# Seven products in five banks with two uses each, the mirrored tile's square first, x added on VectorE for two pairs

## The chip, the cores and the metric

The kernel runs on one core of one Trainium2 chip. The metric is the device time of one execution in microseconds (us). Engines are called by their short names: PE (TensorE, matmuls and transposes), ACT (ScalarE), DVE (VectorE), POOL (GpSimd, which here mostly issues transfers) and SP (SyncE, which issues transfers). Each engine works through its own instructions in order; semaphores tie the engines together. SBUF holds 128 partitions; PSUM, which PE writes to, is used in eight banks of 128 x 512 f32.

## The reference

A sequence x of 2048 rows and 1024 features goes through a Fourier mixing and an MLP, both modulated by a condition c:

```python
mod = (_silu(c) @ w_mod).reshape(c.shape[0], 6, 1, -1)
sa, ca, ga, sb, cb, gb = (mod[:, 0], mod[:, 1], mod[:, 2], mod[:, 3], mod[:, 4], mod[:, 5])
h = _layernorm(x, axis=-1) * (1 + ca) + sa
x = x + ga * _A_ref(h, ...)   # Re(DFT over rows and features)
h = _layernorm(x, axis=-1) * (1 + cb) + sb
x = x + gb * _B_ref(h, ...)
# _B_ref: layernorm, then gelu(y @ w1 + b1) @ w2 + b2, w1 is 1024 x 3584, w2 is 3584 x 1024
```

Everything is f32 at the interface. The part that the change touches is the middle: `x + ga * A`, the two layer norms that follow each other (that of `h` and that inside `_B_ref`), and the operands of the first MLP product.

## The kernel before, in words

The matrix products run in f16 with operands split into a high part (the value rounded to f16) and a low part (the rest). The MLP's products are not taken directly: seven sums and differences of blocks are multiplied for each weight group (a fast matrix product with seven products, m = 0 to 6, in place of eight). So for each group of rows seven operands have to be formed, each as a high and a low f16 tile.

The order of the instructions is fixed by a planner that runs in Python while the kernel is built. Work is cut into `Task`s with an engine, a cost, dependencies and a key. They stand in streams, and the planner always takes the stream head that can start first by its own clocks. `LANDS` says how long after its issue it takes a transfer for done (`("st", "xa")`, an accumulating transfer that adds x, 8.0 us), `LAGS` what it adds for a handover, `due` which stream comes first. These numbers move instructions; they wait for nothing on the chip, where semaphores decide.

The 2048 rows are worked on as 16 row tiles, in 8 pairs b = 0 to 7. Of a pair, tile n = 0 lies in plain order, tile n = 1 in mirrored order, which is read and written by indirect transfers (helpers at L2168 for reading and L2171 for writing, both on POOL). Three pair buffers y and w are used in turn, so pair b uses those of pair b - 3. For each pair (`ln2`):

1. PE makes the Fourier products (L3079 and L3091), DVE brings them to y (L3100, L3105).
2. y is multiplied by ga on DVE (L3211). Then x is added: by an accumulating transfer that POOL issues (mirrored tile through L2168, the other by L3216). For the pairs in `ADDED` (0, 6 and 7) x is loaded into w beforehand (SP at L3164 and POOL through L2168), and DVE multiplies (L3207) and adds (L3208). The sum is stored out, by L2171 for the mirrored tile and on SP at L3223 for the other.
3. The squares on ACT (L3185), DVE's L3233, roots on ACT (L2628, L2629) with a few short DVE steps (L2634 to L2637), DVE's L3237, squares again (L3185), roots again, L3244, and the final L3246 on ACT, which leaves the normalised rows in w.
4. `z_psum` (pairs 0 to 6): PE turns blocks of w into PSUM banks 3 to 7 (L3366), ACT writes the high part of an operand (L3386), DVE the low part (L3414, or L3416 with a factor), and PE adds further blocks into a bank with matmuls by the unit matrix (L3373). For two of the seven, m = 5 and 6, PE subtracts the high part in the bank (L3423) and ACT writes the rest (L3429). For pairs 4 to 6 the operands are kept aside by transfers from POOL (L3405).
5. Pair 7 is turned whole: PE transposes (L3256) into banks 6 and 7, ACT copies out (L3265, L3263).

In `z_psum` the banks before are: 3 and 4 for m = 0 and 1, which are used once; 5 for m = 5; 6 and 7 for m = 3 and 4; and 7 again for m = 2 and once more for m = 6. So bank 7 has three uses in a chain.

Some products of gemm3 (the first MLP matrix; 12 matmuls each at L3860, ACT's L4177 and L4173, DVE's L4183) are put between these steps of the last pairs. After the last turning the two MLP matrices follow, group by group: L3860 is gemm3, L3974 gemm4, and ACT and DVE prepare the weights for them (L2396, L2408, L2422, L3514).

## Time and profile before

| | us |
|---|---|
| three runs, median (lowest to highest) | 1349.69 (1348.94 to 1349.77) |
| the profiled execution, its own time | 1349.1 |
| its span (first to last instruction) | 1347.3 |
| PE busy | 1234.3 |
| DVE busy | 1054.6 |
| ACT busy | 737.2 |
| end of pair 7's last L3246 | 334.1 |
| end of the last turning, L3256 | 344.9 |

1.8 us of the profiled time lie outside the span. A row of a timeline gives the start and the length of an instruction, then its engine, line and tiles, and in brackets how long its engine stood idle before it and what ended that. A row of the groups gives busy time and mean, then the idle time before the group's instructions by what ended it.

### The profile page before, as it was taken

Reading aid. Unit: us, or ns where it says so; the run is one execution under the profiler, and the core shown is the slowest. Engines: PE = TensorE matmul, PEld = TensorE weight load, DVE = VectorE, ACT = ScalarE, POOL = GpSimd, SP = SyncE. Lnnn points to the kernel's source line nnn. Section 1 sums busy time; section 2 is a strip of 40 time slices with the busy share of each in tenths; the row PEclk is TensorE's granted clock in tenths of the full one; section 3 lists DMA queues with packets and bytes.
Section 4 is the critical chain, followed back from the end, with each engine's and each line's share of the span. In section 5 each row is a group of like instructions: output and inputs, shape, how many; then the busy total and the mean of one; then the engine's idle time right before and its main releaser. Section 6 shows DMA issues by size and latency. Waiting matters only on the chain.

```text
span 1347.3 us, 16846 instructions
## 1 busy us (share of the span) xinstructions
PE 1234.3 (92%) x5923; PEld 581.8 (43%) x5923; DVE 1054.6 (78%) x1596; ACT 737.2 (55%) x1207; POOL 248.7 (18%) x380
## 2 busy tenths in 40 slices
PE   3658876679899999999999999999999999999997
PEld 1225434444444444444444444444444444444443
DVE  5789776876688999989899896567777868586785
ACT  4885645878767656474647251366455453526330
POOL 2000123222011000000000001345243242233101
PEclk9689798878899999999999999999999999999999
DMA  9966368776258868483634385968695766585155
GB/s 365 392 213 209 125 219 202 204 256 229 93 201 246 271 181 242 132 252 113 218 107 170 143 331 162 280 229 298 203 315 195 233 229 198 190 290 184 57 175 116
DMA packets 103686, 285.23 MB, mean 212 GB/s; under 512 B 13116, under 2 KB 13132, under 8 KB 101672
## 3 DMA queue, kind: packets, MB, share of 16 engines
q1 hardware_dynamic: 75304, 191.96, 40.9%
q0 software_dynamic: 28288, 92.10, 23.9%
q8 instruction: 48, 0.79, 0.2%
q14 instruction: 46, 0.38, 0.1%
HBM read 199.08 MB, written 84.93 MB: 211 GB/s over the span
## 4 chain that ended last, share of the span: by engine, by line
PE 71%; DVE 2%; ACT 1%; DMA 1%; issue 0%; SPq 0%; DVEq 0%
PE ps L3974 35%; PE ps L3860 35%; DVE arena L4024 1%; DVE arena L2408 1%; DMA arena<-in_w_dram 1%; ACT arena L2396 0%; DVE arena L2422 0%; ACT arena L4173 0%; DVE arena L4076 0%; ACT arena L4014 0%; PE ps L3256 0%; ACT arena L3879 0%; DVE arena L3886 0%; ACT L4173 0%; DVE arena L4071 0%
## 5 line engine op out<-in xcount | busy, mean ns | idle before, releaser
L3860 PE MATMUL ps<-arena 128*128 128x512 f16 x2352 | 514.5, 380 | 1.0 <-ACT arena L3882 1.0
L3974 PE MATMUL ps<-arena 128*128 128x512 f16 x2352 | 510.7, 379 | 2.0 <-DVE arena L4024 1.6
L3860 PEld LDWEIGHTS <-arena 128*128 128x128 f16 x2352 | 230.9, 98 | 281.8 <-issue 7.3
L3974 PEld LDWEIGHTS <-arena 128*128 128x128 f16 x2352 | 230.1, 98 | 280.3 <-issue 2.6
L4024 DVE SCALAR_TENSOR_TENSOR arena<-ps,i4c,arena 128x1024 f32<-128x1024 f32 x179 | 229.4, 1282 | 93.7 <-PE ps L3974 90.0
L2396 ACT ACTIVATE arena<-arena,shc 128x512 f16<-128x512 f32 (+1 forms) x115 | 116.1, 1017 | 129.8 <-DVE arena L2422 76.2
L2408 DVE SCALAR_TENSOR_TENSOR arena<-arena,shc 128x512 f16<-128x512 f32 (+1 forms) x115 | 128.9, 1122 | 35.6 <-ACT arena L2396 35.1
L3744 ACT ACTIVATE arena<-arena 128x512 f32<-128x512 f32 (+4 forms) x159 | 97.2, 613 | 108.1 <-DVE arena L3753 85.2
L2422 DVE TENSOR_TENSOR arena<-arena 128x512 f32<-128x512 f32 (+1 forms) x196 | 149.1, 765 | 3.9
L3879 ACT ACTIVATE arena<-arena,b1s,i1c 128x512 f32<-128x512 f32 x78 | 63.4, 813 | 91.1 <-DVE arena L3886 88.2
L2396 ACT ACTIVATE arena<-arena,s1c 128x512 f16<-128x512 f32 (+1 forms) x70 | 60.9, 886 | 68.1 <-DVE arena L2422 40.2
L3753 DVE TENSOR_TENSOR arena<-arena 128x256 f32<-128x256 f32 x240 | 88.0, 422 | 1.0 <-DMA arena<-in_cre_dram 0.8
L3886 DVE TENSOR_TENSOR arena<-arena,ps 128x512 f32<-128x512 f32 x78 | 53.4, 685 | 43.6 <-PE ps L3860 40.6
L3526 POOL PARTITION_ALL_REDUCE sums<-sums x21 | 9.7, 465 | 419.1 <-DVE sums L3522 407.3
L2408 DVE SCALAR_TENSOR_TENSOR arena<-arena,s1c 128x512 f16<-128x512 f32 (+1 forms) x70 | 65.8, 959 | 7.2 <-ACT arena L2396 7.0
L2408 DVE SCALAR_TENSOR_TENSOR arena<-arena,s2c 128x1024 f16<-128x1024 f32 x49 | 62.1, 1280 | 6.7 <-ACT arena L2396 6.6
L3882 ACT ACTIVATE arena<-ps 128x512 f32<-128x512 f32 x78 | 45.9, 589 | 36.0 <-PE ps L3860 36.0
L3514 ACT ACTIVATE ps<-arena 128x1024 f32<-128x1024 f32 x46 | 46.7, 1015 | 18.8 <-DMA arena<-in_w_dram 11.0
L2396 ACT ACTIVATE arena<-arena,s2c 128x1024 f16<-128x1024 f32 x49 | 55.1, 1138 | 1.5 <-DVE arena L2422 1.5
L3015 PE MATMUL ps<-arena 128*128 128x256 f16 (+5 forms) x297 | 43.8, 296 | 6.6 <-ACT arena L2794 3.2
L3790 POOL DMA_DIRECT2D arena<-in_cim_dram x69 | 38.0, 555 | 53.2 <-ACT arena L3744 28.9
L3185 ACT ACTIVATE arena<-arena,lns 128x1024 f32<-128x1024 f32 x32 | 36.5, 1142 | 20.1 <-DMA arena<-in_x_dram 9.8
(243 smaller groups left out, 1133.8 us busy)
## 6 DMA issues: line engine op xcount, KB each, us to landing
fw<-arena SPq DMA_DIRECT2D x71, 512.0 KB
arena<-fw SPq DMA_DIRECT2D x119, 256.0 KB
arena<-fw SPq DMA_DIRECT2D x49, 512.0 KB
arena<-in_wm_dram SPq DMA_DIRECT2D x32, 512.0 KB
arena<-in_w_dram SPq DMA_DIRECT2D x32, 512.0 KB
arena<-in_cre_dram POOLq DMA_DIRECT2D x64, 256.0 KB
arena<-in_cim_dram POOLq DMA_DIRECT2D x64, 256.0 KB
arena<-in_w_dram SPq DMA_DIRECT2D x56, 256.0 KB
```

Of the source, the lines that this page charges most:

```text
L2396: act.activation(o[m][0], q(j), AF.Copy, **sc)
L2408: dve.scalar_tensor_tensor(o[m][1], q(j), scale, o[m][0], op0=ALU.mult, op1=ALU.subtract)
L2422: dve.tensor_tensor(q(d), q(a), q(b), op=op)
L3514: act.activation(junk, parts[j][0], AF.Square, accum_out=t[:, j : j + 1])
L3744: f = lambda: act.activation(v, v, AF.Square, accum_out=csum[0:pn, n : n + 1])
L3753: return lambda: dve.tensor_tensor(dst[0][:, o::2], src[0][:, o::2], dst[0][:, o::2], op=op)
L3860: pe.matmul(ps.rearrange("p (k t) -> p k t", k=4), w1c[:, m, s, a, d * P : (d + 1) * P], zc(m)[:, b, :, d, :], start=(start and d == 0 and ...
L3879: act.activation(dst, src, AF.Gelu_apprx_tanh, scale=inv, bias=b1s[:, 2 * p + j : 2 * p + j + 1])
L3882: after_pe("act", 0.5, lambda: act.activation(quad(g)[:, n], ps[b], AF.Copy), kp[b])
L3886: after_pe("dve", 0.6, lambda: dve.tensor_tensor(q, q, ps[b], op=ALU.add), kp[b])
L3974: pe.matmul(t[:, j], hidc[:, c_, m, a, k * P : (k + 1) * P], w2c[:, m, c_, w], start=(start and c_ == 0 and n == 0), stop=(c_ == 1 and n = ...
L4024: lambda: dve.scalar_tensor_tensor(dst, ps[b], inv, dst, op0=ALU.mult, op1=ALU.add), kp[b],
```

## The change

The seven operands are now formed in five banks with two uses each: 3 and 4 hold m = 0 and 1, 5 holds m = 5, 6 and 7 hold m = 3 and 4; then m = 6 is made in bank 4 (m1 - m5 + m3) and m = 2 in bank 5 (m5 - m3), each from what still lies there. Four evictions on ACT and four on DVE take the place of seven and three; the path by L3423 and L3429 is gone, and so is the factor -1. Banks 6 and 7 are free once m = 3 and 4 are out, 4 and 5 once m = 6 and 2 are out. Pair 6 leaves `ADDED` and gets x by accumulating transfers. The first squares begin with the mirrored tile. For the planner an addition of x lands after 7.0 us, and not less than 2.8 us after the one before.

In the rows of the change, lines that lie behind the edits carry other numbers: L3216 is now L3218, L3246 L3248, L3256 L3258, L3263 and L3265 are L3265 and L3267, L3366 is L3368, L3373 L3376, L3386 L3389, L3405 L3408, L3414 L3416, L3860 L3843, L3974 L3957, L4173 L4156, L4177 L4160.

What POOL issues for pairs 1 to 4, of before. The rows are, from the top, pair 1's two additions (L2168 the mirrored tile, L3216 the other), pair 1's out-store, pair 2's additions and out-store, pair 3's additions, and pair 4's first:

```order
L2168 DMA arena_65<-in_x_dram,idxm_98 128x1024
L3216 DMA arena_65<-in_x_dram 128x1024
L2171 DMA out_dram<-arena_65,idxm_98 1024x1024
L2168 DMA arena_65<-in_x_dram,idxm_98 128x1024
L3216 DMA arena_65<-in_x_dram 128x1024
L2171 DMA out_dram<-arena_65,idxm_98 1024x1024
L2168 DMA arena_65<-in_x_dram,idxm_98 128x1024
L3216 DMA arena_65<-in_x_dram 128x1024
L2168 DMA arena_65<-in_x_dram,idxm_98 128x1024
```

and of the change:

```order
L2168 DMA arena_65<-in_x_dram,idxm_98 128x1024
L3218 DMA arena_65<-in_x_dram 128x1024
L2168 DMA arena_65<-in_x_dram,idxm_98 128x1024
L3218 DMA arena_65<-in_x_dram 128x1024
L2171 DMA out_dram<-arena_65,idxm_98 1024x1024 x2
L2168 DMA arena_65<-in_x_dram,idxm_98 128x1024
L3218 DMA arena_65<-in_x_dram 128x1024
L2171 DMA out_dram<-arena_65,idxm_98 1024x1024
L2168 DMA arena_65<-in_x_dram,idxm_98 128x1024
```

Pair 2's two additions have moved ahead of pair 1's out-store, and the two out-stores now stand together behind them.

What POOL issues for pairs 5 to 7, of before, where pair 5's additions are followed by its out-store, the load of pair 6's x, pair 6's out-store, and the load of pair 7's x:

```order
L2168 DMA arena_65<-in_x_dram,idxm_98 128x1024
L3216 DMA arena_65<-in_x_dram 128x1024
L2171 DMA out_dram<-arena_65,idxm_98 1024x1024
L2168 DMA arena_65<-in_x_dram,idxm_98 128x1024
L2171 DMA out_dram<-arena_65,idxm_98 1024x1024
L2168 DMA arena_65<-in_x_dram,idxm_98 128x1024
L3405 DMA fzc_67<-arena_65 256x1x512
```

and of the change:

```order
L2168 DMA arena_65<-in_x_dram,idxm_98 128x1024
L3218 DMA arena_65<-in_x_dram 128x1024
L2171 DMA out_dram<-arena_65,idxm_98 1024x1024
L2168 DMA arena_65<-in_x_dram,idxm_98 128x1024
L3218 DMA arena_65<-in_x_dram 128x1024
L2171 DMA out_dram<-arena_65,idxm_98 1024x1024
L3408 DMA fzc_67<-arena_65 256x1x512
L3408 DMA fzc_68<-arena_65 256x1x512
L3408 DMA fzc_72<-arena_65 256x1x512
L2168 DMA arena_65<-in_x_dram,idxm_98 128x1024
```

Pair 6's x is now a pair of additions, L2168 and L3218, behind pair 5's out-store, and the load of pair 7's x stands behind three transfers that keep operands aside.

ACT around the end of pair 7, of before: the last L3246, the evictions of pair 6's operands (L3386, L3429), gelus (L4173), weight preparation (L2396), and the copy of the first turned tile (L3265):

```order
L3246 ACTIVATE arena_65<-arena_65,lns_24_156 128x1024
L4173 ACT_TABLE_LOAD
L4173 ACTIVATE arena_65<-arena_65,b1s_158,i1c_162 128x512
L3386 ACTIVATE arena_65<-ps 128x512
L4173 ACTIVATE arena_65<-arena_65,b1s_158,i1c_162 128x512 x2
L4177 ACTIVATE arena_65<-ps 128x512
L3386 ACTIVATE arena_65<-ps 128x512
L4173 ACTIVATE arena_65<-ps,b1s_158,i1c_162 128x512
L3429 ACTIVATE arena_65<-ps 128x512
L4173 ACTIVATE arena_65<-arena_65,b1s_158,i1c_162 128x512
L2396 ACTIVATE arena_65<-arena_65,s2c_165 128x2x512
L3265 ACTIVATE arena_65<-ps 128x1024
```

and of the change, from the first L3248 of pair 7 to the copy of the second turned tile (L3265):

```order
L3248 ACTIVATE arena_65<-arena_65,lns_24_156 128x1024
L3389 ACTIVATE arena_65<-ps 128x2x512
L4160 ACTIVATE arena_65<-ps 128x512
L3248 ACTIVATE arena_65<-arena_65,lns_24_156 128x1024
L4156 ACTIVATE arena_65<-arena_65,b1s_158,i1c_162 128x512 x2
L3267 ACTIVATE arena_65<-ps 128x1024
L3389 ACTIVATE arena_65<-ps 128x2x512
L4156 ACTIVATE arena_65<-ps,b1s_158,i1c_162 128x512
L3265 ACTIVATE arena_65<-ps 128x1024
```

The copy of the first turned tile (L3267) has moved to the third place behind the last L3248, and pair 6's last eviction stands behind it.

On PE nine, not ten, of the products of gemm3 stand ahead of the last turning; a run of 144 matmuls follows it, where it was 132. The DVE order differs from pair 2's statistics on to the first groups of the MLP, and is the same from there.

The diff:

```diff
--- before.py
+++ after.py
@@ -2187,13 +2187,13 @@
 
     LAGS = {"w": 2.0, "rowl": 1.0, "crawl": 0.5, "row": 0.2, "rowp": 3.0, "ld": 0.5, "z": 1.0, "s": 0.5, "u": 0.3, "op": 0.4, "comb": 0.3, "ln": 0.2}
 
-    LANDS = {"dma": 2.0, "st": 4.0, ("st", "d"): 7.0, ("st", "u"): 5.0, ("st", "s"): 4.0, ("st", "z"): 4.0, ("st", "xa"): 8.0}
+    LANDS = {"dma": 2.0, "st": 4.0, ("st", "d"): 7.0, ("st", "u"): 5.0, ("st", "s"): 4.0, ("st", "z"): 4.0, ("st", "xa"): 7.0}
     LANDS.update({("raw1", g, n): 4.5 for g in (1, 2) for n in range(4)})
     LANDS.update({(n, *k, q): 5.5 for n, k in (("raw2", (0,)), ("early2", ())) for q in range(4)})
     SENT = {("st", "w1s"): 0.7, ("st", "z"): 0.7, ("st", "x1"): 1.4, ("st", "xa"): 1.4}
     PE1 = 0.2165
     PE12 = 12 * PE1
-    bw = [0.0]
+    bw, xa_end = [0.0], [0.0]
     clk = {"pe": 0.0, "dve": 0.0, "act": 0.0, "pool": 0.0, "dma": 0.0}
     done, by, made_by = {}, {}, {}
     streams = {}
@@ -2234,6 +2234,8 @@
                 self.fn()
                 return
             done[self.key] = t + LANDS.get(self.key[:2] if self.eng == "st" and type(self.key) is tuple else self.key, LANDS.get(self.eng, 0.0))
+            if self.eng == "st" and self.key[:2] == ("st", "xa"):
+                done[self.key] = xa_end[0] = max(done[self.key], xa_end[0] + 2.8)
             self.fn()
 
     def chain(*steps):
@@ -3149,7 +3151,7 @@
 
     lns = [mk([P, 6, 2], F32, f"lns{n}") for n in range(3)]
 
-    ADDED = (0, 6, 7)
+    ADDED = (0, 7)
 
     def turned(b):
         return [("zT", b, j) for j in range(5)]
@@ -3227,7 +3229,7 @@
             step("dve", 0.17, lambda: dve.scalar_tensor_tensor(
                 nm, su, -1.0 / D, cm[:, h, k_], op0=ALU.mult, op1=ALU.subtract), ["cm"])
         q = sq(y, w, 1.0, nm)
-        for n in range(2):
+        for n in (1, 0):
             step("act", 1.35, q(n), [x1[n], *wfree])
         for n in range(2):
             step("dve", 1.28, lambda n=n: dve.scalar_tensor_tensor(
@@ -3344,7 +3346,7 @@
 
     def z_psum(b):
         h, k = divmod(b, 4)
-        stage, order = 512 * 184 + 256, (0, 1, 5, 3, 4, 2, 6)
+        stage, order = 512 * 184 + 256, (0, 1, 5, 3, 4, 6, 2)
         due = 100.0 + 22.0 * b
         tag = f"z{b}"
 
@@ -3367,23 +3369,24 @@
 
             return add("seqt", "pe", 0.65, f, [("w", 2 * b + n), *zlast[bk]], ("zT", b, j), due)
 
-        def more(bk, sign, m, deps):
+        def more(bk, sign, ms, deps):
             def f():
-                for a in range(2):
-                    pe.matmul(
-                        PA(512 * bk, (1, 512)), unit16(sign), places((m,), a), start=False, stop=a == 1, skip_group_check=True
-                    )
+                for m in ms:
+                    for a in range(2):
+                        pe.matmul(
+                            PA(512 * bk, (1, 512)), unit16(sign), places((m,), a), start=False, stop=a == 1, skip_group_check=True
+                        )
 
             return add("seqc", "pe", 0.55, f, [*deps, "units"], None, due + 10.0, tag)
 
-        def hi(ms, bk, deps, sc=1.0):
+        def hi(ms, bk, deps):
             n0 = order.index(ms[0])
 
             def f():
                 for m in ms if b > 4 else ():
                     reuse("z", (b - 1, order.index(m)))
                 src = PA(512 * bk, (512, 2), (1, 512)) if len(ms) > 1 else PA(512 * bk, (1, 512))
-                act.activation(places(ms, 0), src, AF.Copy, scale=sc)
+                act.activation(places(ms, 0), src, AF.Copy)
 
             free = [slot("z", (b - 1, n0 + i)) for i in range(len(ms))] if b > 4 else []
             if b == 0 and n0 == 0:
@@ -3393,7 +3396,7 @@
             if b > 4 and n0 == 2:
                 free.append((b - 1, "zlo", (3, 4)))
             if b == 6 and n0 == 0:
-                free.append((4, "zlo", (6,)))
+                free.append((4, "zlo", (6, 2)))
             return add("zh", "act", 0.17 + 0.44 * len(ms), f, [*deps, *free], (b, "zhi", ms), due + 10.0, tag)
 
         def kept_lo(ms, key):
@@ -3405,50 +3408,30 @@
                     store("z", (b, n), lambda dst=dst, v=v: gp.dma_start(dst, v), ("z", b, m), tag=tag)
                 done["z", b, m] = done[key]
 
-        def lo(ms, bk, deps, sc=1.0):
+        def lo(ms, bk, deps):
             key = (b, "zlo", ms)
 
             def f():
                 src = PA(512 * bk, (512, 2), (1, 512)) if len(ms) > 1 else PA(512 * bk, (1, 512))
-                if sc == 1.0:
-                    dve.tensor_tensor(places(ms, 1), src, places(ms, 0), op=ALU.subtract)
-                else:
-                    dve.scalar_tensor_tensor(places(ms, 1), src, sc, places(ms, 0), op0=ALU.mult, op1=ALU.subtract)
+                dve.tensor_tensor(places(ms, 1), src, places(ms, 0), op=ALU.subtract)
                 kept_lo(ms, key)
 
             return add("zl", "dve", 0.12 + 0.58 * len(ms), f, deps, key, due + 10.0, tag)
-
-        def lo_act(m, bk, deps):
-            key = (b, "zlo", (m,))
-            f = lambda: pe.matmul(
-                PA(512 * bk, (1, 512)), unit16(-1), places((m,), 0), start=False, stop=True, skip_group_check=True
-            )
-            c = add("seqc", "pe", 0.35, f, [*deps, "units"], None, due + 10.0, tag)
-
-            def g():
-                act.activation(places((m,), 1), PA(512 * bk, (1, 512)), AF.Copy)
-                kept_lo((m,), key)
-
-            return add("zh", "act", 0.62, g, [c], key, due + 10.0, tag)
 
         t0, t1 = turn_(0, 3, 0, 0), turn_(1, 4, 0, 1)
         t2, t3, t4 = turn_(2, 6, 1, 0), turn_(3, 7, 1, 0), turn_(4, 5, 1, 1)
         k0 = lo((0, 1), 3, [hi((0, 1), 3, [t0, t1])])
-        zlast[3] = zlast[4] = [k0]
-        h5 = hi((5,), 5, [t4])
-        k5 = lo_act(5, 5, [h5])
-        zlast[5] = [k5]
-        c3 = more(6, -1, 0, [t2, k0])
-        c4 = more(7, -1, 5, [t3, k5])
+        zlast[3] = [k0]
+        k5 = lo((5,), 5, [hi((5,), 5, [t4])])
+        c3 = more(6, -1, (0,), [t2, k0])
+        c4 = more(7, -1, (5,), [t3, k5])
         h3 = hi((3, 4), 6, [c3, c4])
         k3 = lo((3, 4), 6, [h3])
-        zlast[6] = [k3]
-        c2 = more(7, -1, 0, [k3])
-        h2 = hi((2,), 7, [c2], -1.0)
-        k2 = lo((2,), 7, [h2], -1.0)
-        c6 = more(7, 1, 1, [k2])
-        h6 = hi((6,), 7, [c6])
-        zlast[7] = [lo_act(6, 7, [h6])]
+        zlast[6] = zlast[7] = [k3]
+        c6 = more(4, 1, (3,), [more(4, -1, (5,), [k0, k5]), k3])
+        c2 = more(5, -1, (3,), [k3])
+        h6 = hi((6, 2), 4, [c6, c2])
+        zlast[4] = zlast[5] = [lo((6, 2), 4, [h6])]
 
     def load_zc(m):
         sp.dma_start(at(O_ZC[m], 4096, F16), zc_d[m].rearrange("p a k c t -> p (a k c t)"))
@@ -4157,7 +4140,7 @@
         return f
 
 
-    zlo = {m: (3, "zlo", ms) for ms in ((0, 1), (5,), (3, 4), (2,), (6,)) for m in ms}
+    zlo = {m: (3, "zlo", ms) for ms in ((0, 1), (5,), (3, 4), (6, 2)) for m in ms}
 
     bank_used = {0: [("y", 7)], 1: [("y", 7)], 2: [("qs", 7)]}
 
```

## The prediction

> **What bounds the kernel now.** I read the page first, then the chain of waits, then the busy time in windows, then the timelines of single engines between 200 and 345 us.
>
> ```profile
> PE 1234.3 (92%) x5923; PEld 581.8 (43%) x5923; DVE 1054.6 (78%) x1596; ACT 737.2 (55%) x1207; POOL 248.7 (18%) x380
> ```
>
> TensorE is busy for 1234.3 us of a span of 1347.3 us: 113 us of idle PE time is all that can be won. The chain (start, length, engine and line, count) says where it isn't:
>
> ```profile
> 333.00 1.13 ACT arena L3246
> ...
> 341.99 0.92 ACT arena L3265
> 342.95 1.97 PE ps L3256 x8
> 344.92 30.22 PE ps L3860 x132
> 375.14 25.99 PE ps L3974 x120
> ...
> 406.48 6.77 DMA arena<-in_w_dram
> ...
> 417.62 31.33 PE ps L3860 x144
> ...
> 485.52 36.30 PE ps L3860 x168
> ```
>
> From 344.92 on the chain is nearly all MLP products. The time is the end of the last turning of a row tile (L3256, 344.92) plus an almost fixed rest. The change works ahead of that point, so its worth is how far this moment moves, and what PE work is pushed behind it. The windows (busy us by engine, PE clock, DMA share, GB/s) show that no engine is full ahead of it, and that two are close to full behind it:
>
> ```profile
> 220.00:240.00 20.00, 11.35 (x67) 7.47 (x66) 13.14 (x26) 13.66 (x24) 6.81 (x5) 0.83 0.88 212
> 280.00:300.00 20.00, 12.04 (x54) 6.32 (x52) 14.92 (x25) 14.94 (x25) 5.99 (x7) 0.76 0.91 327
> 300.00:320.00 20.00, 17.27 (x73) 8.80 (x72) 11.86 (x23) 15.99 (x28) 6.84 (x10) 0.73 0.67 223
> 345.00:380.00 35.00, 35.00 (x156) 15.50 (x155) 29.14 (x38) 25.04 (x32) 0.38 (x1) 0.95 0.29 102
> ```
>
> So the stage is bound by latency: a chain for each row pair, squares on ACT, a row of short DVE steps, ACT again, then the turning on PE. The end of each chain (L3246, both tiles of a pair) is the stage's clock:
>
> ```profile
> 228.90 2.37 ACT L3246 ACTIVATE arena<-arena,lns 128x1024 f32<-128x1024 f32 x2 [0.42 <-DVE lns L3244]
> 244.47 2.37 ACT L3246 ACTIVATE arena<-arena,lns 128x1024 f32<-128x1024 f32 x2 [0.47 <-DVE lns L3244]
> 260.55 2.38 ACT L3246 ACTIVATE arena<-arena,lns 128x1024 f32<-128x1024 f32 x2
> 273.05 2.37 ACT L3246 ACTIVATE arena<-arena,lns 128x1024 f32<-128x1024 f32 x2
> 290.00 2.37 ACT L3246 ACTIVATE arena<-arena,lns 128x1024 f32<-128x1024 f32 x2 [0.55 <-DVE lns L3244]
> 311.12 2.37 ACT L3246 ACTIVATE arena<-arena,lns 128x1024 f32<-128x1024 f32 x2 [0.42 <-DVE lns L3244]
> 332.89 1.24 ACT L3246 ACTIVATE arena<-arena,lns 128x1024 f32<-128x1024 f32 x1
> ```
>
> These are pairs 1 to 7. They follow each other after 15.6, 16.1, 12.5, 17.0, 21.1 and (from the first start of pair 6 to that of pair 7's second tile, less one tile's 1.13 us) 20.6 us. The last two steps are the slowest.
>
> **The change part by part.** Four of its effects have a price, and a fifth is a risk.
>
> A. *Pair 2's x.* POOL issued pair 1's out-store first, and that store waits for an addition to land:
>
> ```profile
> 209.76 1.04 POOL L2171 DMA_INDIRECT out_dram<-arena,idxm  x1 [4.92 <-DMA arena<-in_x_dram,idxm]
> 211.10 1.60 POOL L2168 DMA_INDIRECT arena<-in_x_dram,idxm  x1 [0.30 <-issue]
> 212.10 1.58 POOL L3216 DMA_DIRECT2D arena<-in_x_dram  x1
> 221.57 1.06 POOL L2171 DMA_INDIRECT out_dram<-arena,idxm  x1 [7.89 <-DMA arena<-in_x_dram,idxm]
> 223.98 1.15 ACT L3185 ACTIVATE arena<-arena,lns 128x1024 f32<-128x1024 f32 x1 [6.81 <-DMA arena<-in_x_dram]
> 227.84 0.17 DVE L2634 RECIPROCAL lns<-lns 128x2 f32<-128x2 f32 x1 [6.09 <-ACT lns L2628]
> 229.52 1.01 PE L3373 MATMUL ps<-arena 128*128 128x512 f16 x2 [7.93 <-DVE arena L3416]
> ```
>
> The two additions land 10.5 us (211.10 to 221.57) and 11.9 us (212.10 to 223.98) after their issue. ACT stands 6.81 us at the head of its queue for the second, with pair 1's own last squares behind it; DVE and PE stand still with it. The planner's shorter landing (7.0 us for 8.0) puts both additions ahead of the out-stores, and the squares begin with the tile whose addition goes first; the three edits have this one answer. Its price lies between nothing (the later pairs 3 to 5 are paced by their own landings, and take the lead back) and the whole 6.81 us. I walked the new order with the old durations: pair 1 comes 5 us earlier, pair 2 about 10, but pair 3 only 2 to 6 and pair 4 0 to 4. I take 3 us, near the middle.
>
> By the Trainium skill, "DMA: Bandwidth & Descriptors", section "Anatomy of one DMA — SWDGE (gpsimd) path", a transfer takes 2.0 us and its bytes over 436 KB per us, an estimate of 3.2 us for these 512 KB. The rows above say 10.5 and 11.9 us, so the measurement decides; by the page there would be no wait left in A, and the sum would go to the greater-gain rival below.
>
> B. *Pair 6 without DVE's addition of x.* Pair 7's x is loaded late into pair 4's buffer, and the wait for it holds what is queued behind on DVE:
>
> ```profile
> 297.04 1.23 DVE L3208 SCALAR_TENSOR_TENSOR arena<-arena 128x1024 f32<-128x1024 f32 x1 [4.80 <-DMA arena<-in_x_dram,idxm]
> 298.19 1.22 DVE L3414 TENSOR_TENSOR arena<-ps,arena 128x1024 f16<-128x1024 f32 x1
> 299.32 1.28 DVE L3233 SCALAR_TENSOR_TENSOR arena<-arena,lns 128x1024 f32<-128x1024 f32 x1
> 299.46 1.01 PE L3373 MATMUL ps<-arena 128*128 128x512 f16 x2 [4.06 <-DVE arena L3414]
> ```
>
> Behind it were an eviction that PE waits for (4.06 us) and pair 6's own L3233. In the new order pair 6's products need no x loaded beforehand, and its steps stand among those of pair 5, ahead of pair 7's x; its additions leave POOL behind pair 5's out-store, so not before pair 5's own landing. Two DVE instructions of 1.22 us go (pair 6's addition is a part of the transfer). What replaces them is a landing that the squares wait for. Bounds: nothing, if that landing eats all; and if pairs 6 and 7 came at the pace of pair 4, 12.5 us, (21.1 − 12.5) + (20.6 − 12.5) = 16.7 us. The nearest row is pair 5, which is fed by landings as pair 6 will be and has pair 4's evictions beside it: 17.0 us, about as long as the walk gives. I take 16.4 for both, as DVE and ACT change work as in C: 4.7 + 4.2, or 9 us.
>
> C. *The banks of the seven products.* The groups from 130 to 345 us (busy, mean ns):
>
> ```profile
> L3386 ACT ACTIVATE arena<-ps 128x512 f16<-128x512 f32 (+1 forms) x35 | 26.4, 757 | 12.2 <-PE ps L3373 7.5 <-PE ps L3366 4.8
> L3414 DVE TENSOR_TENSOR arena<-ps,arena 128x1024 f16<-128x1024 f32 x14 | 17.1, 1222 | 6.8 <-ACT arena L3386 6.7
> L3429 ACT ACTIVATE arena<-ps 128x512 f16<-128x512 f32 x14 | 8.3, 590 | 6.5 <-PE ps L3423 4.7 <-PE ps L3366 1.6
> L3416 DVE SCALAR_TENSOR_TENSOR arena<-ps,arena 128x512 f16<-128x512 f32 x7 | 4.8, 689 | 5.4 <-ACT arena L3386 5.4
> ```
>
> ACT's seven evictions of a pair, (26.4 + 8.3) / 7 = 4.96 us, become three double ones (1.01 us, a row below) and a single one (as L3429), 3 × 1.01 + 0.59 = 3.6 us; DVE's 3.13 us become 3 × 1.22 + 0.69 = 4.35 us. Over seven pairs ACT wins 9.4 us and DVE loses 8.5 us (6.1 with B's 2.4 taken off). Two matmuls of L3373 more and two of L3423 fewer for each pair leave PE as it is. Neither engine is full here, so the work itself counts for nothing; what counts is the chain. Banks 6 and 7, which the last pair's turning needs, were the last to come free; now they are free after the second of four evictions, ahead of pair 7's L3246. Before, 10.8 us passed from the last L3246 (334.13) to 344.92. Now the first tile's turning runs under it, and behind the last L3246 stand on ACT two gelus, the eviction of the first turned tile, and then PE's second turning:
>
> ```profile
> 331.99 1.01 ACT L3386 ACTIVATE arena<-ps 128x1024 f16<-128x1024 f32 x1
> ...
> 336.62 1.51 ACT L4173 ACTIVATE arena<-arena,b1s,i1c 128x512 f32<-128x512 f32 x2
> 341.87 1.03 ACT L3265 ACTIVATE arena<-ps 128x1024 f32<-128x1024 f32 x1
> ```
>
> 1.51 + 1.03 + 1.97 + about 0.4 of passing on = 4.9 us, or 5.9 less. If banks 6 and 7 come late after all (the DVE eviction that frees them is of the 1.22 us kind, behind a product's addition), 2 us less is the other bound. I take 5.5.
>
> D. *A product behind the stage.* Nine, not ten, of the first products of gemm3 stand ahead of the last turning; the tenth now runs behind it:
>
> ```profile
> 308.99 3.63 PE L3860 MATMUL ps<-arena 128*128 128x512 f16 x12
> ...
> 327.57 2.75 PE L3860 MATMUL ps<-arena 128*128 128x512 f16 x12
> ```
>
> It costs 2.75 us in full, as the second of these does: nothing covers it. The first shows its upper bound, 3.6 us.
>
> E. *The work behind.* DVE's 6.1 us more, and the weight preparation which a shorter stage leaves over, meet a DVE with 35 − 29.14 = 5.9 us free between 345 and 380 and an ACT with 10. Between nothing and 6.1 us; I take 1, near the lower end, since PE has no stop from 345 to 380 (35.00 of 35 us busy), where its products now find their operands ready.
>
> Sum: −3 − 9 − 5.5 + 2.75 + 1 = −13.75 us on the profiled execution's 1349.1, so 1335.4 us. The median shown, 1349.69, lies 0.6 above that execution: **1336 us**. All bounds at their best give −6.8 − 16.7 − 5.9 + 2.75 = −26.7, at their worst 0 + 0 − 2 + 3.6 + 6.1 = +7.7 us.
>
> **The rivals.** What a measurement can tell from no change is about 0.2%, 2.7 us.
>
> *Slower: the landing of pair 6.* Before, pair 6's x lay ready, and DVE added it in 2.4 us; now its squares wait 11.9 us as those of pair 2 did, which is 9.5 us more, and ACT stands at the head of its queue with pair 5's work behind. Pair 7 keeps its 20.6 us, A is given back: 9.5 − 5.5 + 2.75 + 1 = +7.8, 1357 us. It decides once pair 6 comes over 4.5 us later than before, behind pair 5. For it speak the 6.81 us of pair 2 and the out-store ahead of pair 6's additions on POOL; against it that ACT has other pairs' work in the new order just there. 9%.
>
> *No change: absorbed behind the stage.* PE arrives early and finds its operands unready: the prepared weights need DVE, and the load in the chain at 406.48 (6.77 us) comes no earlier than before. With 6.1 + 6.8 us in place of the 1 of E, −14.75 + 12.9 = −1.9: 1348 us. For it speaks that this load is in the chain; against it that the chain enters it from PE's own results, which come earlier too. 10%.
>
> *A smaller gain: only C.* Landings pace pairs 5 to 7 as they did 2, A is nothing and B worth 2.5: −2.5 − 5.5 + 2.75 + 1 = −4.3, 1345 us. For it speaks that the walk gave pair 4 almost nothing; against it the 4.80 us on DVE, which no landing has to replace. 15%.
>
> *A greater gain.* The landings keep to what the planner assumes, 7 us, A keeps 6.8, B goes to 13: −6.8 − 13 − 5.5 + 2.75 + 1 = −21.6, 1328 us. The 10.5 and 11.9 us speak against it. 10%.
>
> The granted clock of the stage, 0.73 to 0.83 in the windows above, has gaps of PE beside it. The Trainium skill, "TensorE: Matmul & The Clock Gate", section "What's actually happening", ties half speed to an idle window of some 3.4 us; by this rule closing the 4.06 and 7.93 us stops would also shorten the turning, in the direction of this last rival.
>
> That the change doesn't do what it says is excluded by the order: the rows have moved as described.
>
> **How the numbers follow.** The forecast has 56%, with 1329 to 1343 as its own range. Faster: 56 + 15 + 10 = 81%; the same 10%; slower 9%. A range from 1328 to 1347 leaves out the slower case, most of the greater gain and a part of no change, about two in ten.
>
> **What would show it.** A: no wait near 6.8 us of L3185 on additions at pair 2, and pair 2's L3246 near 234. B: pairs 6 and 7 at 16 to 17 us behind one another; DVE's 4.80 us gone. C: last L3246 to the last turning's end about 5 us. D: 144 products in one run behind it. E: stops of PE under 1 us up to 420. The forecast is wrong if the last turning ends later than 335 us, or if PE has stops of several us behind it.

## The result and the profile after

The kernel with the change takes 1342.91 us at the median of seven runs, beside 1349.46 us for the kernel before on the same chips: a ratio of 0.9942, 95% interval 0.9921 to 0.9962. In a second set beside other kernels the ratio was 0.9926 (0.9901 to 0.9952). So the change is faster by 0.6 to 0.7%, some 8 and 10 us; 13.75 us were forecast. The executions that were profiled took 1344.03 us (span 1342.2) and 1336.42 us (span 1334.6): the same order of instructions, with landings that differ. Within one profile a few us therefore say nothing by themselves.

The first line of the page:

```profile
PE 1230.5 (92%) x5923; PEld 579.8 (43%) x5923; DVE 1060.8 (79%) x1601; ACT 731.1 (54%) x1186; POOL 249.8 (19%) x381
```

DVE has 6.2 us more work, as counted (6.1); ACT has 6.1 us less, where 9.4 were counted. The starts of the last step of each pair's chain, in the timeline of ACT of the first profile: pairs 1, 2, 3, 4, 5, 6 and the second tile of pair 7:

```profile
227.03 2.37 ACT L3248 ACTIVATE arena<-arena,lns 128x1024 f32<-128x1024 f32 x2 [0.75 <-DVE lns L3246]
237.52 2.36 ACT L3248 ACTIVATE arena<-arena,lns 128x1024 f32<-128x1024 f32 x2
260.78 2.37 ACT L3248 ACTIVATE arena<-arena,lns 128x1024 f32<-128x1024 f32 x2
274.64 2.38 ACT L3248 ACTIVATE arena<-arena,lns 128x1024 f32<-128x1024 f32 x2 [0.75 <-DVE lns L3246]
292.41 2.38 ACT L3248 ACTIVATE arena<-arena,lns 128x1024 f32<-128x1024 f32 x2 [1.26 <-DVE lns L3246]
303.95 2.37 ACT L3248 ACTIVATE arena<-arena,lns 128x1024 f32<-128x1024 f32 x2 [0.42 <-DVE lns L3246]
330.38 1.24 ACT L3248 ACTIVATE arena<-arena,lns 128x1024 f32<-128x1024 f32 x1
```

Pair 2 leads the old kernel by 7 us (237.52 against 244.47), pair 3 by nothing, pair 4 is 1.6 us behind it; pair 6 leads by 7 again, and pair 7 has kept 2.5 of that. (The stage began 2.1 us later in this execution.) At the end PE's timeline reads:

```profile
331.70 1.04 PE L3258 MATMUL ps<-ident,arena 128*128 128x128 f32 x8
332.58 1.03 PE L3376 MATMUL ps<-arena 128*128 128x512 f16 x4
333.98 1.09 PE L3258 MATMUL ps<-ident,arena 128*128 128x128 f32 x8 [0.38 <-ACT arena L3267]
334.91 31.24 PE L3843 MATMUL ps<-arena 128*128 128x512 f16 x144
```

The last turning ends at 335.07, 3.5 us behind the last L3248 (331.62), where it was 10.8 us. That moment came 9.9 us earlier than before; the span is shorter by 5.1. So what follows the turning has grown by 4.7 us. The run of gemm3 that begins it took, before:

```profile
344.72 30.43 PE L3860 MATMUL ps<-arena 128*128 128x512 f16 x132
```

The 144 matmuls of the change took only 0.8 us more than these 132, because the granted clock of the window from 345 to 380 us is 1.00 now, where it was 0.95. Most of the growth, 3.3 us, are stops of PE further on, where the kernel before had one of 0.96 us:

```profile
371.77 18.29 PE L3957 MATMUL ps<-arena 128*128 128x512 f16 x84 [0.43 <-ACT arena L3997]
390.38 13.11 PE L3957 MATMUL ps<-arena 128*128 128x512 f16 x60 [0.33 <-ACT arena L3997]
...
409.13 23.61 PE L3843 MATMUL ps<-arena 128*128 128x512 f16 x108 [0.46 <-ACT arena L3865]
433.77 2.75 PE L3843 MATMUL ps<-arena 128*128 128x512 f16 x12 [1.02 <-ACT arena L3865]
438.50 5.34 PE L3843 MATMUL ps<-arena 128*128 128x512 f16 x24 [1.98 <-ACT arena L3865]
```

They come to 4.2 us, 1.2 of it before 420 us, and ACT ends each: with evictions (L3997, L3865) that stand in its queue behind the weight preparation. DVE is the fuller engine there, as the windows show (busy us of PE, PEld, DVE, ACT):

```profile
345.00:380.00 35.00, 34.57 (x162) 15.61 (x160) 32.77 (x42) 26.98 (x32) 1.79 (x3) 1.00 0.34 122
```

DVE was busy for 29.14 of these 35 us before, and is for 32.77 now.

To compare kernels I cut each profile at four moments: the end of pair 0's last normalisation (L3246, or L3248 in the change), of pair 4's, of pair 7's, and of the last turning; what follows to the end of the span is "the rest". All in us, one profile each, with the ratio of the runs to the kernel before on the same chip:

| kernel | pair 0 to 4 | pair 4 to 7 | tail | rest | ratio (95%) |
|---|---|---|---|---|---|
| before | 69.5 | 58.7 | 10.8 | 1002.4 | 1 |
| the change | 69.0 | 54.6 | 3.5 | 1007.1 | 0.9942 (0.9921 to 0.9962) |
| change_again | 67.4 | 51.9 | 3.5 | 1005.9 | 0.9926 (0.9901 to 0.9952) |
| undo_banks | 68.1 | 56.8 | 9.8 | 1003.7 | 0.9962 (0.9947 to 0.9977) |
| undo_pair6 | 69.4 | 58.2 | 4.7 | 1004.3 | 0.9975 (0.9959 to 0.9992) |
| undo_landing | 68.8 | 59.1 | 7.5 | 1005.8 | 0.9997 (0.9979 to 1.0015) |
| undo_squares | 77.4 | 53.6 | 3.5 | 1007.6 | 0.9979 (0.9964 to 0.9994) |
| only_banks | 76.1 | 52.9 | 3.5 | 1006.6 | 0.9970 (0.9948 to 0.9992) |
| only_squares | 61.3 | 62.4 | 13.5 | 997.9 | 0.9946 (0.9927 to 0.9964) |
| banks_and_squares | 67.6 | 61.8 | 4.7 | 1005.1 | 0.9968 (0.9952 to 0.9985) |
| pool_later | 69.8 | 50.4 | 3.5 | 1006.9 | 0.9911 (0.9886 to 0.9936) |
| weights_and_pool_later | 69.0 | 49.2 | 5.8 | 1004.7 | 0.9896 (0.9868 to 0.9924) |
| y3_early | 67.9 | 57.1 | 3.9 | 1007.0 | 0.9924 (0.9898 to 0.9949) |
| all_y_early | 70.9 | 56.9 | 5.6 | 1009.9 | 0.9997 (0.9978 to 1.0017) |

The columns of a row, with its start (204.9 to 209.8 us for the end of pair 0), make up its span. The two rows of the change show how far one order varies: 1.6 and 2.7 us in the first two columns, nothing in the tail, 1.2 us in the rest. Differences of that size between other rows say nothing. One of the twelve executions of all_y_early, a slow one, took 3286.34 us and is not in its ratio.

### The profile page after: what moved, and what is told of

It reads as the page before. It is cut to its first block, busy times and chain, and to the rows that moved or that the text cites. A ratio compares the mean times of both kernels' runs of the same rounds, so it can differ in the third digit from the quotient of the medians.

```text
span 1342.2 us, 16824 instructions
## 1 busy us (share of the span) xinstructions
PE 1230.5 (92%) x5923; PEld 579.8 (43%) x5923; DVE 1060.8 (79%) x1601; ACT 731.1 (54%) x1186; POOL 249.8 (19%) x381
## 4 chain that ended last, share of the span: by engine, by line
PE 66%; DVE 4%; ACT 2%; DMA 2%; issue 1%; POOL 0%; SPq 0%; DVEq 0%; ACTq 0%; POOLq 0%
PE ps L3957 34%; PE ps L3843 32%; DVE arena L2410 2%; DMA arena<-in_w_dram 1%; ACT arena L2398 1%; DVE arena L2424 1%; DVE arena L4007 1%; DMA fzc<-arena 1%; DVE arena L3869 0%; ACT ps L3497 0%; ACT arena L3862 0%; DVE arena L4059 0%; DVE arena L3304 0%; ACT arena L4156 0%; ACT arena L3997 0%
## 5 line engine op out<-in xcount | busy, mean ns | idle before, releaser
L3843 PE MATMUL ps<-arena 128*128 128x512 f16 x2352 | 513.6, 380 | 5.5 <-ACT arena L3865 3.5
L3957 PE MATMUL ps<-arena 128*128 128x512 f16 x2352 | 510.9, 379 | 2.7 <-DVE arena L4007 1.6
L3843 PEld LDWEIGHTS <-arena 128*128 128x128 f16 x2352 | 230.4, 98 | 285.2 <-issue 7.6
L3957 PEld LDWEIGHTS <-arena 128*128 128x128 f16 x2352 | 230.0, 98 | 281.3 <-issue 3.7
L3862 ACT ACTIVATE arena<-arena,b1s,i1c 128x512 f32<-128x512 f32 x78 | 63.4, 813 | 89.7 <-DVE arena L3869 86.8
L3865 ACT ACTIVATE arena<-ps 128x512 f32<-128x512 f32 x78 | 46.0, 589 | 36.1 <-PE ps L3843 36.0
```

Source lines behind the costliest of these rows:

```text
L3843: pe.matmul(ps.rearrange("p (k t) -> p k t", k=4), w1c[:, m, s, a, d * P : (d + 1) * P], zc(m)[:, b, :, d, :], start=(start and d == 0 and ...
L3862: act.activation(dst, src, AF.Gelu_apprx_tanh, scale=inv, bias=b1s[:, 2 * p + j : 2 * p + j + 1])
L3865: after_pe("act", 0.5, lambda: act.activation(quad(g)[:, n], ps[b], AF.Copy), kp[b])
L3957: pe.matmul(t[:, j], hidc[:, c_, m, a, k * P : (k + 1) * P], w2c[:, m, c_, w], start=(start and c_ == 0 and n == 0), stop=(c_ == 1 and n = ...
```

## The experiments

**Undoing one part.** Four kernels, each the change with one part put back; my theory (1) was that the banks carry nearly the whole gain.

```diff
# undo_banks: the function z_psum of the kernel before
# undo_pair6
-    ADDED = (0, 7)
+    ADDED = (0, 6, 7)
# undo_landing: ("st", "xa"): 8.0, and
-            if self.eng == "st" and self.key[:2] == ("st", "xa"):
-                done[self.key] = xa_end[0] = max(done[self.key], xa_end[0] + 2.8)
# undo_squares
-        for n in (1, 0):
+        for n in range(2):
             step("act", 1.35, q(n), [x1[n], *wfree])
```

> The changed kernel with z_psum as before (seven evictions on ACT, bank 7 with three uses); the x additions, the landing rule and the order of squares stay changed. Theory 1 (the gain is the freed banks 6 and 7: the tail from the last normalisation of pair 7 to the last turning fell from 10.8 to 3.5 us): the tail goes back to about 10 us and the time to 1348 to 1351 us. Rival (the gain comes from the earlier pairs, by the x additions): it stays within 2 us of 1343.

> The changed kernel with x added on DVE for pairs 0, 6 and 7, as before. Theory 1 (pair 6 came 11.5 us after pair 5 instead of 21.1, but pair 7 then waited for a product's weights on PE and for the all-reduce on POOL, so that it is held by these and not by pair 6): within 3 us of 1343. Rival (pair 6's addition is worth the 9 us forecast): 1350 to 1353 us.

> The changed kernel with the planner's landing of an x addition at 8.0 us and without the 2.8 us rule. Theory 1 (the early order of pair 2's additions was given back by pair 4): within 2.5 us of 1343, pair 4's normalisation within 2 us of 274.6. Rival (the forecast's term A): 1346 us, with pair 4 at 277 or later.

> The changed kernel with the first squares in the order plain tile, mirrored tile. Theory 1: the squares wait 1 to 2 us more at pairs 1 to 6 and the time stays within 2.5 us of 1343. Rival (the mirrored tile's addition goes first, so each pair gains the 2.8 us between the two landings): 1346 us or more.

*undo_banks*: 1346.85 us, 0.9962. The tail is back at 9.8 us, as theory 1 had it. PE of this kernel, where the last turning again comes in pieces, behind the eviction of a rest (L3431):

```profile
336.20 0.60 PE L3258 MATMUL ps<-ident,arena 128*128 128x128 f32 x4
337.18 0.66 PE L3258 MATMUL ps<-ident,arena 128*128 128x128 f32 x4 [0.38 <-ACT arena L3431]
...
340.26 1.04 PE L3258 MATMUL ps<-ident,arena 128*128 128x128 f32 x8
```

But half of the gain or more stays (0.38%), so the banks are not nearly the whole of it, and the time lies between what theory 1 and its rival expected; by the times alone, whose intervals overlap with those of the change, a loss is not shown.

*undo_pair6*: 1347.5 us, 0.9975. Theory 1 fails: the stretch from pair 4 to 7 takes 58.2 us again, as before the change, and 4 to 7 us are lost (0.9975 against 0.9942 and 0.9926). The rival's 9 us is not reached either. And DVE's wait for pair 7's x, on which the forecast built, is nearly gone although pair 6 is added on DVE again (0.27 us where it was 4.80):

```profile
292.56 1.23 DVE L3210 SCALAR_TENSOR_TENSOR arena<-arena 128x1024 f32<-128x1024 f32 x1 [0.27 <-DMA arena<-in_x_dram,idxm]
```

Pair 6 still comes 19.7 us behind pair 5, where it was 11.5 in the change. What holds it, I did not trace.

*undo_landing*: 1352.34 us, 0.9997: the whole gain is gone, though the edit touches only numbers by which the planner orders. Pair 4 is not late: its L3246 starts at 271.97, so the rival's 277 is wrong (theory 1 had 274.6 within 2 us, but this execution's stage also began 2.5 us earlier; from pair 0 to 4 it is 68.8 us against 69.0 and 67.4). Neither theory has the time. So it is not the forecast's term A. The loss comes later: 59.1 us from pair 4 to 7, and a tail of 7.5 us. Pair 6 comes 24.5 us behind pair 5. In the new order a product of gemm3 stands on PE long before its weights have landed, and ACT's copy of its result stands ahead of pair 6's last L3246 (starts at 313.63), whose inputs DVE had ready at 309.7:

```profile
308.44 4.66 PE L3841 MATMUL ps<-arena 128*128 128x512 f16 x12 [10.47 <-DMA arena<-fw]
313.13 0.60 ACT L4158 ACTIVATE arena<-ps 128x512 f32<-128x512 f32 x1 [4.30 <-PE ps L3841]
```

Behind pair 7, in ACT's order of this kernel the table load, an eviction, three gelus and a copy stand between the last L3246 and the copy of the first turned tile (L3265):

```profile
331.08 2.37 ACT L3246 ACTIVATE arena<-arena,lns 128x1024 f32<-128x1024 f32 x2
333.88 1.02 ACT L3387 ACTIVATE arena<-ps 128x1024 f16<-128x1024 f32 x1 [0.43 <-PE ps L3374]
334.92 1.28 ACT L4154 ACT_TABLE_LOAD   x1
336.22 1.52 ACT L4154 ACTIVATE arena<-arena,b1s,i1c 128x512 f32<-128x512 f32 x2
...
338.83 1.00 ACT L3265 ACTIVATE arena<-ps 128x1024 f32<-128x1024 f32 x1
```

*undo_squares*: 1349.97 us, 0.9979. Theory 1 fails here too, and the rival's time comes, though not by the 2.8 us for each pair that it gave as the reason: pair 4 is 8 us later (77.4 instead of 69.0 us). In this kernel's order POOL has pair 1's out-store ahead of pair 2's additions, as before the change. In undo_landing, which has the squares' new order and the old landing time, they do stand ahead. So it is this edit, not the landing time, that moves them, and ACT stands at its queue's head even longer (timelines of POOL and ACT):

```profile
212.80 1.03 POOL L2171 DMA_INDIRECT out_dram<-arena,idxm  x1 [5.05 <-DMA arena<-in_x_dram,idxm]
214.14 1.60 POOL L2168 DMA_INDIRECT arena<-in_x_dram,idxm  x1 [0.30 <-issue]
...
226.72 1.15 ACT L3187 ACTIVATE arena<-arena,lns 128x1024 f32<-128x1024 f32 x1 [8.28 <-DMA arena<-in_x_dram]
```

In the change the same two places read:

```profile
208.95 1.88 POOL L2168 DMA_INDIRECT arena<-in_x_dram,idxm  x1 [2.34 <-PE ps L3368]
211.38 0.91 POOL L3218 DMA_DIRECT2D arena<-in_x_dram  x1 [0.56 <-issue]
212.60 1.04 POOL L2171 DMA_INDIRECT out_dram<-arena,idxm  x1 [0.30 <-issue]
...
220.87 1.15 ACT L3187 ACTIVATE arena<-arena,lns 128x1024 f32<-128x1024 f32 x1 [2.31 <-DMA arena<-in_x_dram]
```

**The change again, and the banks alone; two waits at pair 7.** With theory 1 down for three parts, I asked what the banks do alone, and where pair 7 loses what pair 6 has won (25.3 us from pair 6's end to pair 7's, 20.6 before). The change's rows there, PE, ACT and DVE:

```profile
304.10 4.45 PE L3843 MATMUL ps<-arena 128*128 128x512 f16 x12 [2.01 <-DMA arena<-fw]
308.38 0.60 PE L3368 MATMUL ps<-ident,arena 128*128 128x128 f32 x4
308.82 1.03 PE L3376 MATMUL ps<-arena 128*128 128x512 f16 x4
```

```profile
309.45 1.02 ACT L3389 ACTIVATE arena<-ps 128x1024 f16<-128x1024 f32 x1 [3.13 <-PE ps L3376]
310.37 0.59 ACT L4160 ACTIVATE arena<-ps 128x512 f32<-128x512 f32 x1
310.85 1.15 ACT L3187 ACTIVATE arena<-arena,lns 128x1024 f32<-128x1024 f32 x1
```

```profile
325.90 0.15 DVE L3513 TENSOR_SCALAR sums<-sums 128x1 f32<-128x1 f32 x1 [2.23 <-POOL sums L3509]
...
326.80 0.16 DVE L2636 RECIPROCAL lns<-lns 128x2 f32<-128x2 f32 x1
```

A product waits on PE for its weights; pair 6's turning, an eviction on ACT and pair 7's first square are queued behind one another after it. Later DVE waits for an all-reduce on POOL, with pair 7's short steps behind.

```diff
# change_again: the change; only_banks: the kernel before with the new z_psum
# pool_later: the change with
-        r.append(Task("pool", 0.5, all_, [r[-1].key]))
+        r.append(Task("pool", 4.5 if key == ("s2", 0) else 0.5, all_, [r[-1].key]))
# weights_and_pool_later: that, and
+    LANDS.update({("w1", g, m): 6.0 for g in (0, 1) for m in (2, 3)})
```

> The change itself, beside the next kernels on one chip. All theories: 5 to 10 us under the kernel before; its row of pair ends falls as in the first profile, pair 7 about 25 us behind pair 6.

> The kernel before with the new z_psum alone (five banks with two uses; x for pairs 0, 6, 7 on DVE, squares and landing as before). Theory 1 (the banks shorten the tail by 5 to 7 us, whatever the rest does): last turning within 6 us of the last normalisation, 1343 to 1346 us. Rival (the order that the planner makes of it decides the tail, and the parts only work together): tail over 8 us and 1348 to 1351 us.

> The change, where the planner takes the all-reduce of the second weight's scale for 4.5 us long instead of 0.5, so that pair 7's last short DVE steps stand ahead of the scale's. Theory 2 (pair 7 is late by 2 to 3 us since DVE waits for POOL's all-reduce, 2.23 us, ahead of these steps): pair 7's end and the last turning 2 to 3 us earlier, 2 us under the change. Rival (the wait is covered): within 1 us of the change.

> As the last, and the planner takes four weight loads of gemm3's first products for 6.0 us long instead of 2.0, so that these products stand behind the turning of pair 6 and pair 7's squares stand together. Theory 2 (the 26 us between pairs 6 and 7 come from a product that waits 2.0 us for its weights on PE, with pair 6's turning and then ACT's eviction and pair 7's squares behind it): pair 7 follows pair 6 after 18 to 21 us, 4 to 6 us under the change. Rival (pair 7 is held by the landing of its own x): pair 7 stays at 24 us or more behind pair 6, within 2 us of the change.

*change_again*: 1343.54 us, 0.9926; pair 7 came 22.6 us behind pair 6, not the 25 expected, and the waits were 1.05 us for the weights and 2.23 us for POOL. So 1 us of the 2.7 by which the step of the first profile is longer goes with the landing of those weights.

*only_banks*: 1347.49 us, 0.9970. Theory 1 is right on the tail and misses the time by 1.5 us; the rival is wrong on the tail and near on the time. The tail is 3.5 us without any other part, and the stretch from pair 4 to 7 is 52.9 us, short as in the change, with pair 6 still added on DVE; of DVE's wait for x 0.24 us are left in it. But the stretch from pair 0 to 4 takes 76.1 us:

```profile
230.29 2.37 ACT L3246 ACTIVATE arena<-arena,lns 128x1024 f32<-128x1024 f32 x2 [0.75 <-DVE lns L3244]
240.50 2.36 ACT L3246 ACTIVATE arena<-arena,lns 128x1024 f32<-128x1024 f32 x2
262.25 2.37 ACT L3246 ACTIVATE arena<-arena,lns 128x1024 f32<-128x1024 f32 x2
279.12 2.37 ACT L3246 ACTIVATE arena<-arena,lns 128x1024 f32<-128x1024 f32 x2 [1.67 <-DVE lns L3244]
...
336.79 1.09 PE L3256 MATMUL ps<-ident,arena 128*128 128x128 f32 x8 [0.38 <-ACT arena L3265]
```

The new banks lose 6.6 us at pairs 1 to 4, win 5.8 and 7.3 us behind them, and lose 4.2 again in the rest.

*pool_later*: 1341.21 us, 0.9911, 2.3 us under change_again on the same chip, with intervals that overlap. The short steps now run ahead of the wait, which is 0.70 us; pair 7 follows pair 6 after 21.1 us.

*weights_and_pool_later*: 1340.43 us, 0.9896. Pair 7 follows pair 6 after 18.4 us, in the 18 to 21 expected, so the two waits, and not pair 7's x, held it; 1.4 us of this is only moved, as pair 6 now follows pair 5 after 13.1 us, not 11.7. The time is 3.1 us under change_again, less than the 4 to 6 expected and again within the intervals; the tail has grown to 5.8 us. PE has no stop from the last turning to 490 us, although the run behind it is now of 156 matmuls. Against the kernel before it is the fastest that I ran: 1.04% (0.76 to 1.32%).

**The squares, and what they repay.** Theory 3: the new banks cost pairs 1 to 4 some 7 us, and the squares' order repays it.

```diff
# only_squares: the kernel before; banks_and_squares: only_banks, each with
-        for n in range(2):
+        for n in (1, 0):
             step("act", 1.35, q(n), [x1[n], *wfree])
# y3_early: weights_and_pool_later, with the due time of pair 3's two evictions to y (all_y_early: of pairs 3 to 7)
-        add("yev", "dve", 0.72, up, deps, ("y", b), due)
+        add("yev", "dve", 0.72, up, deps, ("y", b), due - 60.0 if b == 3 else due)
```

> The kernel before with the first squares beginning with the mirrored tile, nothing else changed; in its order POOL issues pair 2's additions ahead of pair 1's out-store, as in the change. Theory 3 (the squares' order is worth 7 to 9 us for pairs 1 to 4, by the two profiles with the new banks that lack it): pair 4's normalisation 4 to 8 us earlier than in the kernel before, time 1342 to 1346 us for a before of 1350. Rival (as the forecast's A: the lead is given back by pair 4; the order only repays what the new banks cost there): pair 4 within 3 us of before, time within 3 us of it.

> The kernel before with the new banks and the new order of squares; pair 6 and the landing as before. Theory 3 (the new banks cost pairs 1 to 4 about 7 us, 76 instead of 69 from pair 0's end to pair 4's, and the squares' order repays it): 67 to 70 us there, time 1343 to 1346 us. Rival (7 us lost come from something else): 74 us or more, 1347 us or more.

> As weights_and_pool_later, and the planner gets pair 3's two evictions to y with an earlier due time, so that DVE does them ahead of pair 2's step of the squares. Theory 3 (the lead of pair 2 is lost since y of pair 3 is evicted 14 us later than before on DVE, and with it its product with ga and its additions): pair 3 follows pair 2 after 14 to 17 us instead of 23, 3 to 6 us under weights_and_pool_later. Rival (pairs 3 to 5 are paced by the landings of the additions whatever their issue): pair 5's end unchanged within 2 us, time too.

> The same for the evictions to y of pairs 3 to 7. Theory 3: as y3_early or 1 to 3 us better, since every pair's additions go out earlier. Rival: the evictions delay the short steps behind them, no better than weights_and_pool_later.

*only_squares*: 1345.89 us beside 1352.78, 0.9946 (0.9927 to 0.9964): within the intervals, one line does as much as the whole change. Pair 4 ends 61.3 us after pair 0, 8.2 us less than before; theory 3 had 4 to 8. Some of it is lost on the way, and with the old banks the tail is longer (13.5 us, with a product more ahead of the last turning; the rest is 4.5 us shorter, 2.6 of it this product):

```profile
206.28 1.88 POOL L2168 DMA_INDIRECT arena<-in_x_dram,idxm  x1 [2.35 <-PE ps L3366]
208.72 0.91 POOL L3216 DMA_DIRECT2D arena<-in_x_dram  x1 [0.57 <-PE ps L3366]
209.93 1.04 POOL L2171 DMA_INDIRECT out_dram<-arena,idxm  x1 [0.30 <-issue]
...
265.36 1.23 ACT L3246 ACTIVATE arena<-arena,lns 128x1024 f32<-128x1024 f32 x1
...
326.67 2.36 ACT L3246 ACTIVATE arena<-arena,lns 128x1024 f32<-128x1024 f32 x2
```

*banks_and_squares*: 1347.12 us, 0.9968. Pair 0 to 4 takes 67.6 us, in the 67 to 70 expected. The four corners agree: old banks 69.5 and 61.3 us, new banks 76.1 and 67.6 us, so the squares save about 8 us with either, and the banks cost about 6.5 us with either, as long as the other two edits are as before. With these two it is otherwise: undo_banks, which has the old banks, the squares' new order and both other edits, lies at 68.1 and not at 61, and the change with the new banks at 69.0 and 67.4. There the banks cost nothing that these profiles can tell. But the stretch from pair 4 to 7 is 61.8 us here, and the total is no better than that of the banks alone, 1 us over what theory 3 had.

*y3_early*: 1342.01 us, 0.9924; *all_y_early*: 1352.08 us, 0.9997. My reason for the 6.5 us (the later eviction of pair 3's y on DVE) fails: it was done at 218.68 and 222.55 instead of 227.87 and 230.59 in weights_and_pool_later, and pair 3 still came 24.4 us behind pair 2; its product with ga stayed where it was in DVE's order (second tile at 239.56, and at 240.40 there). The rival fails too: pair 5 ends 90.7 us behind pair 0, and 86.8 there. Moving all the evictions costs the whole gain. What exactly in the order delays pair 3 with the new banks stays open. DVE's load is not the answer: between 205 and 260 us it is busy for 43.93 us in the change and 40.33 before, but for 39.75 in only_banks, which loses the 6.6 us.

## Why the prediction was right, and where its sizes were wrong

The sign, the place (ahead of 345 us) and the range held: 1342.91 lies in 1328 to 1347, between the forecast and the rival of a smaller gain, and nearer to the latter. The forecast was too far by 4 to 6 us. The range held because it was wide; the terms inside it did not come as they were added. By the forecast's own signs of being wrong the first profile is at the edge: its last turning ended at 335.07 (335 was the limit), and the stops of PE behind it, though none is longer than 1.98 us, come to 4.2. In the second profile the turning ended at 328.69. Step by step:

- *What bounds the kernel* held: the time followed that moment and the rest, which is less fixed than was thought (1002.4 us before, 1007.1 and 1005.9 with the change).
- *A*, 3 us. Pair 2's lead came as described (7 us, the 6.81 us wait now 2.31) although its second addition still took 9.5 us to land (211.38 to 220.87). By the Trainium skill, "DMA: Bandwidth & Descriptors", section "Anatomy of one DMA — SWDGE (gpsimd) path", an estimate for it is 3.2 us. The trace differs from the page, and the rows decide. The lead was given back by pair 4: 0.5 and 2.1 us are left in the two profiles. The step that failed is "the three edits have this one answer". The order of squares alone moved POOL's additions and alone is worth 8 us at pair 4; the landing time did nothing there. What gave the lead back is shown only in part. With pair 6 and the landing rule as before, the new banks cost this stretch 6.5 us, which the forecast had not counted ("the work itself counts for nothing"). But without them the lead is gone all the same once the other two edits are in (undo_banks, 68.1 us).
- *B*, 9 us. From pair 4 to 7 the change saves 4.1 and 6.8 us. Pair 6 came 11.5 us behind pair 5, faster than the 16.4 assumed, and pair 7 25.3 and 22.6 us behind pair 6, slower. The mechanism was wrong in part: the wait of 4.80 us for pair 7's x also goes with x on DVE for pair 6 (only_banks 0.24, undo_pair6 0.27 us). The waits that took its place, for a product's weights and for POOL's all-reduce, were not among those named; weights_and_pool_later brought pair 7 to 18.4 us.
- *C*, 5.5 us. Right in mechanism and mis-sized: 7.3 us in both profiles, and the tail is 3.5 us with the new banks alone and 9.8 without them. The banks do not give it in every order: undo_landing has them and a tail of 7.5 us. The seven operands use banks 4 and 5 twice and banks 3, 6 and 7 once, not each of five twice, and 6 and 7 come free behind the third of pair 6's four evictions, not the second as the forecast has it: ACT writes its high part at 329.00, DVE its low part from 330.03 to 331.26, and PE begins the turning at 331.70. The chain is the one that was counted, two gelus, the copy and the second turning; this took 1.09 us, not the 1.97 of the row before. The granted clock was 0.50 there before (343 to 347 us) and is 1.00 in the change. Before, PE had stood for 1.99 us ahead of it; in the change only 0.38 us. By the Trainium skill, "TensorE: Matmul & The Clock Gate", section "What's actually happening", an idle window of about 3.4 us halves the clock. The trace agrees on the half. It does not show that the stop just ahead of an instruction decides: in all_y_early the same turning took 1.09 us right behind a stop of 2.62 us, and the clock was 0.50 only after it (340.3 to 343 us).
- *D* and *E*, 2.75 + 1. The rest grew by 4.7 and 3.5 us. D is 12 matmuls of 0.216 us, 2.6 us, but the full clock behind the turning gave 1.8 us of it back, which the forecast did not have. The stops came to 1.2 us instead of "under 1 us up to 420", and to 3.0 us more behind that.
- *The rivals.* The slower one (pair 6's landing) did not come: pair 6 came 11.5 us behind pair 5, and only pair 2 followed its forerunner more closely (10.5 us). The smaller gain came nearest in time, for another reason than the one given: more of B is there than its 2.5 us. Of "absorbed behind the stage" about 2 us came, in stops of PE beyond the 1 us of E.

So the step that failed is the sum itself: A, B and C were added as independent terms. The bank edit that gives C, made alone, takes 6.6 us from A's stretch and moves B's by itself (52.9 us alone, 61.8 with the squares, 58.7 before), and numbers that only the planner reads (undo_landing) are worth as much as the whole change. Which part of each new order does this is traced for a few waits only.

## What to carry to other kernels

Where a planner orders the work, price an edit in the order that results, not on the old timeline: undoing any of the four edits moved stretches that it was not made for, their gains did not add, and one line alone (0.9946) gave, within the intervals, as much as all of them. Look for waits whose transfer or all-reduce a planner takes for too short: with two such numbers raised the kernel ran at 0.9896 beside 0.9926, with intervals that still overlap. In an in-order queue the question is what stands behind a waiting instruction; most of the waits traced here were of this kind.

## What the runs showed that I had not expected

One kernel's profiled executions differ by 7.6 us in span (1342.2 and 1334.6) with the same order: 2.0 us in the start of the stage, 4.4 us from there to pair 7's end, 1.2 us in the rest. In the kernel before, the long runs of the MLP further back in the chain take 36.26 us each, one like the other. So in these two profiles most of the spread arises ahead of the last turning, where transfers are waited for.
